# Attention and gated MLP on one core: v's normalization moves from GpSimd to ScalarE, row sums come from the exponential's accumulator, products get a third PSUM bank, and the hand-written order is replaced

## The chip, the core and the metric

The kernel runs on one core of a Trainium2 chip. The metric is device microseconds of one execution. Engines are named as in the profile: PE (TensorE matmul) and PEld (its weight load), DVE (VectorE), ACT (ScalarE), POOL (GpSimd), SP (SyncE, which issues nearly all DMAs).

## The reference

Four batches, 8 heads, 768 positions, 64 columns a head. Attention keeps the first 4 positions (sinks) and a window of 128; its result, 512 columns a row, goes through a gated MLP with a spatial product:

```python
keep = is_sink | in_window
scores = np.where(keep, scale * (q @ k.T), -1e9)
a = np.exp(scores - scores.max(-1)); a = a / (a.sum(-1) + 1e-9)
x = a @ v                                   # heads joined: 512 columns
h = np.maximum(x @ w_in, 0.0)
u, v = h[..., :512], h[..., 512:]
v_n = (v - v.mean(-1)) / np.sqrt(v.var(-1) + 1e-6)
v_s = np.einsum('ts,bsd->btd', w_spatial, v_n) + b_spatial[None, :, None]
out = (u * v_s) @ w_out
```

## The kernel before

A batch has six tiles of 128 positions (`NT`), and each tile two halves of four heads. For each half, `scores` multiplies the queries with the keys of the tile and of the tile before it, 260 columns a head with 2 sink columns on either side (PE into four banks `sc`); DVE adds the mask and takes the row's minimum `nm` (L781); ACT takes the exponential with `nm` as its bias (L786). `weights` splits the result into two fp16 parts `p high` and `p low`, which DMAs turn (`turn high`, `turn low`, L852). `attend` multiplies them with v (`av`: three matmuls for each pair of blocks, L900 to L902). The value tile has a 65th column of ones, so column 65 of each head's product is the row sum. `divide` then reads that column, adds 1e-9, inverts (L908, L909) and multiplies (L910) on DVE. One `av` tile takes two banks, one for each half.

The joined 512 columns `x` are split into two fp16 parts and turned. `v_half` multiplies them with the second half of w_in (`ps_v`), takes the relu, then on DVE mean and variance (`v stats`), on POOL the power -0.5 (`v root`, L1012), and subtracts the mean and multiplies by the root in one instruction (`v norm`, L1015), on POOL or DVE; `vn high` and `vn low` split the result. `u_half` makes u (`ps_u`), `s_piece` the spatial product (`ps_s`), DVE adds the bias (`gate`, L1072), `times` multiplies by u, and `o_piece` multiplies with w_out (`ps_o`). All these products, and the PE transposes `pt` of the first tiles, share two PSUM banks (`mm`). The first two tiles (`crossed`) are computed in fp32, while w_in is still being decoded from its 64-bit form (`w_in`: L548, L550, L553, L556).

Nothing is scheduled by a program: `fast_path` collects 1799 pieces, and the text `ORDER` names them in the sequence in which they are written out, each with its engine (P, d, a, p, S). Each engine runs its own pieces in that sequence. A number behind P (`120P20`) puts that many stand-in matmuls of 248 columns on `ident` ahead of the piece (`warm`, L440). The times given to `plan.add` are not used by the program. In what follows a *score group* is one piece `score`: there are 48.

Of the kernel before, what the change touches and what calls it, by code (L numbers as in the profile page):

```python
# [6 lines left out]
F32 = mybir.dt.float32  # L7
# [6 lines left out]
ALU = mybir.AluOpType  # L14
# [39 lines left out]
def general_path(tc, wf, qk, v, w_in, w_sp, b_sp, w_out, out):  # L54

    nc = tc.nc
    with (
# [46 lines left out]
        for b in range(B):  # L104
            xT = gc.tile([P, DM // P, S], F32, name="g_xT")
            vsb = gc.tile([P, NT, H, D + 1], F32, name="g_v")
            nc.sync.dma_start(vsb, v[b].rearrange("(c p) h d -> p c h d", p=P))
            x = gc.tile([P, NT, DM], F32, tag="g_xg", name="g_x")
            for h in range(H):
# [5 lines left out]
                for t in range(NT):  # L115
# [25 lines left out]
                    for c in range(NT):  # L141
                        nc.tensor.matmul(po[:, :D], prT[:, c, :], vsb[:, c, h, :D],
                                         start=(c == 0), stop=(c == NT - 1))
# [69 lines left out]
BANKS = {"sc": 4, "av": 1, "mm": 2}  # L213
# [8 lines left out]
def cost(e, n, two=False, pointer=False):  # L222

    if e == "a":
        return 0.1 + n / 1200 + (0.1 if pointer else 0)
    if e == "d":
        return 0.085 + n / (960 if two else 1920) + (0.05 if pointer else 0)
    return 0.17 + n * 0.0018 if two else 0.14 + n * 0.001
# [5 lines left out]
116S 120P20 121d 123d 125d 117S 118p 257p 156p 119p 107S 108a 109a 21S 126a 127d 128a 111S 112a 110d 132P6:131  # L234
137d 139d 122a 124a 129P3 135d 22a 23d 133d 113a 136a 24d 25p 209p 114d 155S 159P1:131 164d 162d 140a 166d 130a
138a 134a 42S 141P2 160d 43a 44d 165a 115S 45d 46p 14S 131P 16d 163a 173P 180d 178d 174d 167a 161a 168P 142a 26a
176d 170P 143P 17d 15a 18p 208S 212P 144d 213d 215d 181a 217d 219d 179a 28S 30d 169a 47a 48d 313p 171a 154S 157p
0S 2d 177a 175a 216a 29a 31d 32p 214a 3d 184P15 218a 220a 185a 223a 1a 4p 182P 228P 233d 221a 183d 224d 235d 231d
229d 7S 9d 8a 35S 37d 236a 36a 207S 210a 230a 10d 11p 234a 256S 232a 239a 240p 225d 172P 145P 186P 187d 237a 49S
260P5 261d 38d 146a 50a 51d 39p 311S 314a 267d 33a 12a 188P9 189a 58S 263d 222S 265d 266a 241d 158d 211d 190a  # L240
268a 226S 255S 147P 148a 262a 264a 271a 269a 191d 52d 53p 272p 34d 276P 279d 258a 280a 227P 283d 284a 281d 282a
277d 192P 259d 273d 315d 312S 316P 319d 323d 321d 242S 317d 238S 243P 244d 245P23 278a 285a 289p 332P 287a 288p
5a 360S 6d 54a 40a 41d 27d 55d 270S 274S 275P 324a 322a 318a 339d 320a 193a 325a 286S 290S 246a 503S 327a 19a
333d 337d 340a 338a 334a 199P 326S 335d 247d 361p 364P 329p 328d 330S 336a 343a 344p 341a 13d 20d 504p 505p 345p
367d 368a 365d 200a 371d 369d 291P 56S 359S 292d 149d 342S 150p 151p 201P 346S 202a 380P 381d 550p 366a 370a 372a
373a 377p 57S 387d 383d 385d 382a 384a 194d 195p 293P 386a 294a 295d 375a 196p 248P 376d 508P 515d 513d 331P 509d
511d 374S 63a 64d 378S 249a 152a 388a 391a 203P 392d 549S 347P 389a 390S 393p 204a 153d 394S 348d 516a 250d 510a
512a 205P 206a 522P 296P 527d 523d 525d 349P 362a 363d 65a 251p 524a 66d 379P 529d 528a 526a 514a 517d 519p 297a
298d 652p 299p 197a 350a 530a 351d 67a 198p 553P 560d 561a 531a 558d 559a 556d 554d 555a 303P 395P 304d 533d 501S
506a 68d 557a 252p 253a 254p 567P 574d 568d 569a 396d 570d 603p 300p 572d 59S 69a 70d 352P 353a 518S 507d 520S  # L250
602S 562a 564p 307P 308a 547S 354d 355p 356p 397P 606P 398a 399d 493S 551a 573a 60S 71a 552d 521P 532S 613d 607d
571a 600S 534S 301a 309P 310d 72d 575a 576a 302d 611d 609d 400P 401a 402d 604a 409P 614a 563S 535P 536d 357a 578p
622P 625d 627d 623d 709p 403p 358p 629d 61S 73a 410a 74d 407P 408d 548a 537a 626a 605d 305P 538d 565S 404p 651S
566P 655P 405a 624a 612a 610a 608a 617a 615a 306d 618d 83S 85d 619d 86d 579S 406p 415P 658d 62S 416d 420P 577S
84a 87p 494a 628a 630a 631a 656d 657a 660d 662d 601a 633a 634p 495a 421d 422p 635d 580P 581d 582a 413P 414d 671P
672d 676d 539S 540P 417p 418a 419d 75S 663a 678d 77d 423p 424d 496d 76a 78d 79p 541a 661a 88a 708S 1658a 411P
412a 583d 425P 497S 91S 620S 674d 498a 499a 675a 426d 93d 427d 616S 94d 80a 92a 81d 679a 584S 428a 500d 429d 659a
677a 664a 666a 632S 89d 667p 636S 90a 430P 431d 673a 758p 95p 432p 668d 712P 719d 717d 718a 715d 713d 621P 542d
680a 684p 585P 586a 587d 706S 446P 447d 448p 682a 683d 710a 82p 728P 731d 733d 649S 735d 99S 101d 720a 96a 596P
597a 449a 450d 102d 653d 100a 734a 433a 637P 434d 592P 593a 594P 595a 732a 654d 103p 104a 105d 106p 755S 756a  # L260
441P 442d 729d 451P 736a 650a 98a 757S 761P 900S 901a 730a 665S 97d 443d 588p 669S 589d 590a 638d 711d 759a 760d
444d 438P 739a 740d 452d 453d 502a 670P 737a 741d 681S 685S 439a 902a 903d 440S 435P 738S 1055S 714a 716a 723a
764d 445d 454a 686P 721a 725p 762d 455d 766d 767a 742S 1005S 768d 436a 437S 894S 687d 724p 726S 456P 765a 769a
763a 457d 458d 459a 777P 770d 780d 722S 949S 890S 460d 784d 772a 773p 904p 1061p 639p 778d 782d 785a 781a 783a
953p 477P 743P 467P 774p 478d 468d 469d 598P 905p 775S 771S 479d 480a 895a 779a 788a 470p 471d 908P 913d 911d
599d 909d 915d 896a 897d 543p 640p 1003S 707a 914a 591d 910a 464P 465a 786d 790d 481d 922P 472P 473d 688a 912a
916a 951a 727P 789d 927d 923d 952d 925d 689d 926a 891a 917a 919p 950a 1006a 466S 641S 929d 930a 482P 483d 484d
744d 947S 954a 461P 462a 898S 474p 475d 956P 959d 963d 957d 476d 961d 485a 791S 787S 924a 906d 486d 463S 1009p
544d 745p 776P 1057S 690S 955d 892a 1007a 920S 642P 487P 928a 931p 643a 644d 746d 933p 970P 977d 488a 489S 747S
# [82 lines left out]
def begin(nc, pool, qk, v, w_in, b_sp):  # L352
# [893 lines left out]
```

## Time and profile before

| | |
|---|---|
| median of 3 runs | 401.75 us (401.38 to 401.91) |
| the profiled execution | 401.43 us, of which the profiled span is 399.6 us |
| PE busy | 387.3 us, 97% of the span |
| DVE, ACT, POOL busy | 312.4, 250.8, 210.5 us |
| granted TensorE clock | 0.999 of full speed |

Busy times are sums over the whole span; a matmul's length includes its passage through the array, so matmuls overlap and the pace is read from one start to the next.

### The profile page before, as it was taken

Reading aid. Unit: us, or ns where it says so; the run is one execution under the profiler, and the core shown is the slowest. Engines: PE = TensorE matmul, PEld = TensorE weight load, DVE = VectorE, ACT = ScalarE, POOL = GpSimd, SP = SyncE. Lnnn points to the kernel's source line nnn. Section 1 sums busy time; section 2 is a strip of 40 time slices with the busy share of each in tenths; the row PEclk is TensorE's granted clock in tenths of the full one; section 3 lists DMA queues with packets and bytes.
Section 4 is the critical chain, followed back from the end, with each engine's and each line's share of the span. In section 5 each row is a group of like instructions: output and inputs, shape, how many; then the busy total and the mean of one; then the engine's idle time right before and its main releaser. Section 6 shows DMA issues by size and latency. Waiting matters only on the chain. (4 is left out here: it accounts for less than half of the span.)

```text
span 399.6 us, 9923 instructions
## 1 busy us (share of the span) xinstructions
PE 387.3 (97%) x3697; PEld 276.4 (69%) x3697; DVE 312.4 (78%) x924; ACT 250.8 (63%) x553; POOL 210.5 (53%) x237
## 2 busy tenths in 40 slices
PE   7999998998999999999999999999999998999995
PEld 4785866686786774677777666777768666486773
DVE  3899999879888787989798897989896998342421
ACT  3999897877879476688796979888621131101010
POOL 4463596874552526454515478499666392720000
PEclk9999999999999999999999999999999999999999
DMA  6999999999895998869888979899799653001021
GB/s 194 384 284 218 196 183 230 256 251 219 205 228 135 242 188 192 214 153 144 165 173 210 207 186 267 143 189 147 168 237 232 185 175 85 27 2 53 2 80 57
DMA packets 137733, 70.96 MB, mean 178 GB/s; under 512 B 112080, under 2 KB 125392, under 8 KB 137680
## 3 DMA queue, kind: packets, MB, share of 16 engines
q1 hardware_dynamic: 136864, 70.02, 77.9%
q8 instruction: 30, 0.49, 0.5%
q10 hardware_dynamic: 816, 0.26, 0.3%
q14 instruction: 23, 0.19, 0.2%
HBM read 36.71 MB, written 6.29 MB: 108 GB/s over the span
## 5 line engine op out<-in xcount | busy, mean ns | idle before, releaser
L529 PE MATMUL ps_s<-wsp,vn 128*128 128x256 f16 x864 | 100.3, 273 | 0.7 <-ACT ob L1112 0.7
L786 ACT ACTIVATE pexp<-pexp,nm 128x260 f32<-128x260 f32 (+1 forms) x192 | 85.3, 484 | 18.6 <-DVE nm L781 18.2
L529 PEld LDWEIGHTS <-vn 128*128 128x128 f16 x864 | 83.1, 98 | 14.1 <-issue 2.2
L511 POOL TENSOR_TENSOR p<-pexp,p 128x1024 f16<-128x1024 f32 (+2 forms) x43 | 54.8, 1280 | 44.7 <-ACT p L495 35.7
L529 PE MATMUL ps_u<-xT,win 128*128 128x256 f16 x576 | 68.8, 273 | 1.6 <-DVE g L1072 1.1
L1099 PE MATMUL ps_o<-wout,g 128*128 128x512 f16 x276 | 62.9, 379 | 0.7 <-ACT ob L1112 0.7
L529 PEld LDWEIGHTS <-win 128*128 128x128 f16 x576 | 55.0, 98 | 11.4 <-issue 3.9
L529 PE MATMUL ps_v<-win,xT 128*128 128x512 f16 x264 | 60.5, 380 | 0.1
L1099 PEld LDWEIGHTS <-g 128*128 128x128 f16 x276 | 26.3, 98 | 30.1 <-issue 1.6
L776 PE MATMUL sc<-kring 64*128 64x260 f16 (+3 forms) x480 | 44.7, 312 | 1.3 <-DMA kring<-qk_t 1.2
L529 PEld LDWEIGHTS <-xT 128*128 128x128 f16 x264 | 24.8, 98 | 28.5 <-issue 1.5
L495 ACT CAST p<-pexp 128x32 f16<-128x32 f32 (+2 forms) x69 | 42.7, 639 | 2.7 <-DMA pT<-p 2.0
L1072 DVE SCALAR_TENSOR_TENSOR g<-ps_s,b_bc 128x256 f32<-128x256 f32 x48 | 20.2, 420 | 28.7 <-PE ps_s L529 28.6
L1015 POOL TENSOR_SCALAR vr<-vr,mv,rs 128x512 f32<-128x512 f32 x18 | 38.4, 2136 | 0.8
L1076 POOL TENSOR_TENSOR g<-g,u 128x256 f32<-128x256 f32 x22 | 17.4, 792 | 33.8 <-DVE g L1072 33.1
L1049 ACT ACTIVATE u<-ps_u 128x256 f32<-128x256 f32 x34 | 12.8, 378 | 34.2 <-PE ps_u L529 34.1
L900 PE MATMUL av<-vring,pT 128*128 128x65 f16 x328 | 34.2, 194 | 0.0
L901 PE MATMUL av<-vring,pT 128*128 128x65 f16 x328 | 34.1, 193 | 0.0
L902 PE MATMUL av<-vring,pT 128*128 128x65 f16 x328 | 34.1, 193 | 0.0
L511 DVE TENSOR_TENSOR p<-pexp,p 128x1024 f16<-128x1024 f32 (+2 forms) x33 | 27.0, 820 | 6.3 <-ACT p L495 6.2
L900 PEld LDWEIGHTS <-pT 128*128 128x128 f16 x328 | 30.3, 97 | 1.8 <-issue 0.8
L1084 DVE SCALAR_TENSOR_TENSOR g<-g,g 128x256 f16<-128x256 f16 x48 | 23.0, 484 | 10.0 <-POOL g L679 7.1
(144 smaller groups left out, 693.4 us busy)
## 6 DMA issues: line engine op xcount, KB each, us to landing
vraw<-v_s SPq DMA_DIRECT2D x30, 260.0 KB, 4.1
raw<-qk_t SPq DMA_DIRECT2D x12, 512.0 KB, 4.1
out<-ob SPq DMA_DIRECT2D x23, 256.0 KB, 2.3
kring<-qk_t SPq DMA_DIRECT2D x11, 512.0 KB, 5.6
dec<-w_in SPq DMA_DIRECT2D x8, 512.0 KB, 8.1
pexp<-w_in SPq DMA_DIRECT2D x8, 512.0 KB, 4.4
wsp<-w_sp_t SPq DMA_DIRECT2D x6, 384.0 KB, 4.1
dec<-w_out SPq DMA_DIRECT2D x4, 512.0 KB, 4.6
```

The costliest lines, as they stand in the source:

```text
L495: nc.scalar.copy(o, x)
L511: eng[e].tensor_tensor(out=o, in0=x, in1=hi, op=ALU.subtract)
L529: nc.tensor.matmul(o, a, m, start=(i == 0), stop=(i == n - 1))
L776: nc.tensor.matmul(view(h + q)[0], qq[:, hp, 1, 2:], keys, start=(j == 0), stop=(j == len(pairs) - 1))
L786: nc.scalar.activation(po, po, AF.Exp, bias=nm()[:, q:q + 1], scale=-1.0)
L900: nc.tensor.matmul(o[:, h], ph, vh, start=(t < 2 and j == 0), stop=False)
L901: nc.tensor.matmul(o[:, h], ph, vl, start=False, stop=False)
L902: nc.tensor.matmul(o[:, h], pl, vh, start=False, stop=(j == nb - 1 and (t < 2 or h == HH - 1)))
L1015: eng[e].tensor_scalar(vr(), vr(), vals["mv", i][:, 0:1], vals["rs", i], op0=ALU.subtract, op1=ALU.mult)
L1072: nc.vector.scalar_tensor_tensor(out=g(), in0=tl("ps_s", i)[:, :TC], scalar=G_S, in1=b_bc[:, t0:t0 + TC], op0=ALU.mult, op1=ALU.add)
L1084: plan.add("g low", r, b, "d", cost("d", TC, True), lambda e: nc.vector.scalar_tensor_tensor(out=g2()[:, 1], in0=g2()[:, 0], scalar=-2.0 * ...
L1099: nc.tensor.matmul(o, lead, wout[:, w, d, :], start=(d == 0 and j == 0), stop=(d == KC - 1 and j == 2))
```

## The change

1. The value tiles lose their column of ones (64 columns a head in place of 65). The exponential (now L783) also gives its row sum through ScalarE's accumulator into `sums`. The inverse of the sums is a DVE piece of its own, `den`, which needs no product; `divide` is one multiplication.
2. One `av` tile now fills a single bank with both halves. The bank so freed goes to the products: `mm` has three.
3. `v norm` runs on ACT (`Identity` with a scale and a bias per row) or on DVE, never on POOL. For it, POOL makes `nb`, minus mean times root, behind the root.
4. `ORDER` is replaced as a whole (1815 pieces: 24 `den` more, 8 copies of the ones column fewer). Its stand-ins are 73 in place of 84. It moves work between engines: `v norm` goes from 18 on POOL and 6 on DVE to 20 on ACT and 4 on DVE.
5. At the start, the first keys and queries come in four DMAs of two heads' pairs, alternating between SP's and ACT's queues, in place of two.

```diff
-BANKS = {"sc": 4, "av": 1, "mm": 2}
+BANKS = {"sc": 4, "av": 1, "mm": 3}
...
-116S 120P20 121d 123d 125d 117S 118p 257p 156p 119p 107S 108a 109a 21S 126a 127d 128a 111S 112a 110d 132P6:131
...
+114S 118P16 119d 121d 122a 21S 22a 23d 115S 110S 116p 209p 258p 117p 155p 125d 111a 123d 124a 24d 130P8:141 133d
...
-    st.vring = vring = pool.tile([P, NV, 2, H, D + 1], F16, name="vring")
-    nc.gpsimd.memset(vring[:, :, 0, :, D:], 1.0)
-    nc.gpsimd.memset(vring[:, :, 1, :, D:], 0.0)
...
+    st.vring = vring = pool.tile([P, NV, 2, H, D], F16, name="vring")
...
-            "av": ("av", lambda name: ps_all.tile([P, 2, 512], F32, tag="av", name=name, bufs=1)),
+            "av": ("av", bank("av")),
...
-                nc.scalar.activation(po, po, AF.Exp, bias=nm()[:, q:q + 1], scale=-1.0)
+                k = HH * hf + q
+                nc.scalar.activation(po, po, AF.Exp, bias=nm()[:, q:q + 1], scale=-1.0,
+                                     accum_out=small_tile("sums", (b, t), H)[:, k:k + 1])
...
+            def inverse(e):
+                den = small_tile("sums", (b, t), H)
+                nc.vector.tensor_scalar(den, den, 1e-9, None, op0=ALU.add)
+                nc.vector.reciprocal(den, den)
+
             def divide(e):
-                o = tl("av", (b, t))[:, :, :HH * (D + 1)].rearrange("p s (h d) -> p s h d", h=HH)
-                den = small.tile([P, 2, HH], F32, tag="den", name="den")
-                nc.vector.tensor_scalar(den, o[:, :, :, D], 1e-9, None, op0=ALU.add)
-                nc.vector.reciprocal(den, den)
-                nc.vector.tensor_tensor(out=tl("x", (b, t)), in0=o[:, :, :, :D],
-                                        in1=den.unsqueeze(3).to_broadcast([P, 2, HH, D]), op=ALU.mult)
+                den = small_tile("sums", (b, t), H)
+                nc.vector.tensor_tensor(out=tl("x", (b, t)).rearrange("p s h d -> p (s h) d"),
+                                        in0=tl("av", (b, t)).rearrange("p (h d) -> p h d", h=H),
+                                        in1=den.unsqueeze(2).to_broadcast([P, H, D]), op=ALU.mult)
...
             def root(e):
-                nc.gpsimd.tensor_tensor(out=vals["rs", i], in0=vals["rs", i], in1=mhalf, op=ALU.pow)
+                rs = vals["rs", i]
+                nc.gpsimd.tensor_tensor(out=rs, in0=rs, in1=mhalf, op=ALU.pow)
+                vals["nb", i] = small.tile([P, 1], F32, tag="nb", name="nb")
+                nc.gpsimd.tensor_scalar(vals["nb", i], vals["mv", i][:, 0:1], rs, -1.0, op0=ALU.mult, op1=ALU.mult)
 
             def norm(e):
-                eng[e].tensor_scalar(vr(), vr(), vals["mv", i][:, 0:1], vals["rs", i], op0=ALU.subtract, op1=ALU.mult)
+                if e == "a":
+                    nc.scalar.activation(vr(), vr(), AF.Identity, bias=vals["nb", i], scale=vals["rs", i])
+                else:
+                    nc.vector.tensor_scalar(vr(), vr(), vals["mv", i][:, 0:1], vals["rs", i], op0=ALU.subtract, op1=ALU.mult)
...
-            plan.add("v norm", r, b, "dp", {"d": 0.46, "p": 0.75}, norm, [("st", i)], [("vr", i)], shared=True)
+            plan.add("v norm", r, b, "ad", {"a": 0.61, "d": 0.47}, norm, [("st", i)], [("vr", i)], shared=True)
...
-            for e, hs in ((nc.sync, slice(0, HP // 2)), (nc.scalar, slice(HP // 2, HP))):
-                e.dma_start(kring[:, 0, hs, :, 2:], qk[0, 0, :, hs])
+            for h in range(HP):
+                (nc.sync, nc.scalar)[h % 2].dma_start(kring[:, 0, h:h + 1, :, 2:], qk[0, 0, :, h:h + 1])
```

What the engines' own sequences look like at the places that matter below: first POOL, at the first normalizations of v, before the change. `rs` is the root, `vr` the tile that is normalized, `p` the low part of the softmax weights of one half.

```order
L1012 TENSOR_TENSOR rs<-rs,mhalf 128x1
L1015 TENSOR_SCALAR vr<-vr,mv,rs 128x512
L748 COPY kring<-ksink 128x4x2
L511 TENSOR_TENSOR p_0_130<-pexp,p_0_130 128x1024
L1012 TENSOR_TENSOR rs<-rs,mhalf 128x1
L1015 TENSOR_SCALAR vr<-vr,mv,rs 128x512
L511 TENSOR_TENSOR p_1_131<-pexp,p_1_131 128x1024
```

The same place of POOL in the change:

```order
L509 TENSOR_TENSOR p_1_130<-pexp,p_1_130 128x1024
L1015 TENSOR_TENSOR rs<-rs,mhalf 128x1
L1017 TENSOR_SCALAR nb<-mv,rs 128x1
L740 COPY ksink<-kring 128x16
L744 COPY kring<-ksink 128x4x2 x2
L502 TENSOR_SCALAR p_0_129<-pexp 128x1024
L509 TENSOR_TENSOR vn<-vr,vn 128x512
L509 TENSOR_TENSOR p_0_129<-pexp,p_0_129 128x16
L1015 TENSOR_TENSOR rs<-rs,mhalf 128x1
L1017 TENSOR_SCALAR nb<-mv,rs 128x1
```

The wide instruction behind each root has gone from POOL, a narrow one has come, and a root still stands behind the low part of a half's weights. On ACT the wide one appears between exponentials, as `vr<-vr,nb,rs` (in the change):

```order
L783 ACTIVATE pexp,sums<-pexp,nm 128x260 x2
L493 CAST p_1_130<-pexp 128x1024
L493 CAST p_1_130<-pexp 128x2x16
L1021 ACTIVATE vr<-vr,nb,rs 128x512
L783 ACTIVATE pexp,sums<-pexp,nm 128x128 x4
L1021 ACTIVATE vr<-vr,nb,rs 128x512
L493 CAST p_0_129<-pexp 128x512
```

ACT's queue before the change holds, between exponentials of the same batch, only relus, casts and scaled copies. In the change an ACT instruction that needs POOL's `nb` stands ahead of the next batch's first exponentials (128 columns).

## Rows read from the trace of the kernel before

**Rows 1.** The page: the span, PE's busy time, and its clock in 40 slices.

```profile
span 399.6 us, 9923 instructions
...
PE 387.3 (97%) x3697; PEld 276.4 (69%) x3697; DVE 312.4 (78%) x924; ACT 250.8 (63%) x553; POOL 210.5 (53%) x237
...
PEclk9999999999999999999999999999999999999999
```

**Rows 2.** Waits of PE: who waited for whom: us in total, times, longest.

```profile
PE sc L440 <- POOL ident masks.py:199: 1.7, 1, 1.7
PE sc L776 <- DMA kring<-qk_t: 1.2, 2, 1.0
PE ps_u L529 <- DVE g L1072: 1.1, 1, 1.1
PE pt L815 <- ACT pexp L786: 1.0, 1, 1.0
PE ps_o L1099 <- ACT ob L1112: 0.7, 1, 0.7
PE ps_s L529 <- ACT ob L1112: 0.7, 1, 0.7
PE ps_u L529 <- ACT u L1049: 0.4, 1, 0.4
```

**Rows 3.** Timeline of PE, 102 to 110 us: start, us, instruction.

```profile
102.62 1.15 PE L776 MATMUL sc<-kring 64*128 64x260 f32 x8
103.70 0.28 PE L894 MATMUL av<-vsink,pT 96*128 96x260 f16 x1
103.82 0.20 PE L900 MATMUL av<-vring,pT 128*128 128x65 f16 x1
...
104.55 2.75 PE L529 MATMUL ps_v<-win,xT 128*128 128x512 f16 x12
107.14 2.13 PE L529 MATMUL ps_s<-wsp,vn 128*128 128x256 f16 x18
109.20 1.15 PE L776 MATMUL sc<-kring 64*128 64x260 f32 x8
```

**Rows 4.** Stand-in matmuls: count, busy us, mean ns, idle before.

```profile
L440 PE MATMUL pt<-ident 128*128 128x248 f16 x52 | 6.4, 270 | 0.0
L440 PE MATMUL sc<-ident 128*128 128x248 f16 x25 | 5.0, 382 | 1.7 <-POOL ident masks.py:199 1.7
L440 PE MATMUL av<-ident 128*128 128x248 f16 x7 | 1.1, 271 | 0.0
```

**Rows 5.** Two stretches: length, then busy PE, PEld, DVE, ACT, POOL.

```profile
6.00:49.00 43.00, 41.79 (x377) 30.86 (x376) 39.83 (x138) 39.72 (x86) 18.93 (x21) 1.00 1.05 267
49.00:94.00 45.00, 42.59 (x446) 31.19 (x446) 39.01 (x123) 37.49 (x79) 34.36 (x28) 1.00 1.09 239
```

**Rows 6.** Timeline of ACT: an accumulator read; an exponential and a cast.

```profile
81.92 0.37 ACT L1049 ACTIVATE u<-ps_u 128x256 f32<-128x256 f32 x1
82.19 0.62 ACT L606 ACTIVATE junk<-vraw 128x512 bf16<-128x512 f32 x1
82.71 0.19 ACT L606 ACTIVATION_READ_ACCUMULATOR junk<-vraw 128x1 f32 x1
82.80 0.61 ACT L495 CAST x<-x 128x512 f16<-128x512 f32 x1
...
119.65 0.51 ACT L786 ACTIVATE pexp<-pexp,nm 128x260 f32<-128x260 f32 x1
120.05 0.61 ACT L495 CAST vn<-vr 128x512 f16<-128x512 f32 x1
```

**Rows 7.** Groups of POOL by shape: busy us, mean ns.

```profile
L511 POOL TENSOR_TENSOR p<-pexp,p 128x1024 f16<-128x1024 f32 x20 | 42.2, 2109 | 24.1 <-ACT p L495 24.0
L1015 POOL TENSOR_SCALAR vr<-vr,mv,rs 128x512 f32<-128x512 f32 x18 | 38.4, 2136 | 0.8
L1012 POOL TENSOR_TENSOR rs<-rs,mhalf 128x1 f32<-128x1 f32 x24 | 18.6, 774 | 15.5 <-DVE rs L1009 15.2
```

More of the change, by code (lines that the diff above doesn't have):

```diff
@@ L420, in fast_path @@
             nc.gpsimd.memset(t[:, 4 * HH], 0.0)
-        vsink = [const.tile([96, HH, D + 1], F16, name=f"vsink{i}") for i in range(4)]
+        vsink = [const.tile([96, HH, D], F16, name=f"vsink{i}") for i in range(4)]
         win = const.tile([P, 2, KC, DFF], F16, name="win")
@@ L437, in g @@
                 o = tl(*key[:2])
-                o = o[:, key[2], :248] if key[0] == "av" else o[:, :248]
+                o = o[:, :248]
                 for _ in range(count):
@@ L555, in decode @@
                 [("dec", i)], [("w32", i)], shared=True)
-            plan.add(name, step, 0, "p", 1.27, lambda e: nc.gpsimd.tensor_tensor(
+            plan.add(name, step, 0, "p", 1.23, lambda e: nc.gpsimd.tensor_tensor(
                 out=ci(), in0=ci(), in1=tl("wtmp", i), op=ALU.add), [("wtmp", i)], [("w32", i)])
@@ L614, in check_ranges @@
                 i = ("again", t)
-                load("v check", last, 0, "vraw", i, lambda t=t: v[0, t * P:(t + 1) * P], 260)
+                load("v check", last, 0, "vraw", i, lambda t=t: v[0, t * P:(t + 1) * P], 256)
                 sum_v("v check", last, 0, t, i)
@@ L790, in scores @@
                 keys = [(f"kslot{kslot(0, 0)}", (0, 0), (0, hf))]
-            plan.add("score", i, b, "PE", (0.78 if t else 0.45) if b >= B16 else 1.08 if t else 0.75, product, keys, banks)
+            plan.add("score", i, b, "PE", (0.86 if t else 0.53) if b >= B16 else 1.17 if t else 0.74, product, keys, banks)
             for q in range(n):
@@ L916, in attend @@
             else:
-                plan.add("av", i, b, "PE", 0.0306 * 3 * n + (0.105 if t > 1 else 0.0), product,
+                plan.add("av", i, b, "PE", 0.0302 * 3 * n + (0.104 if t > 1 else 0.0), product,
                          [("pT", i)] + vkeys + ([(f"vsink{vsk}", b)] if t > 1 else []), [("av", (b, t), hf)])
@@ L920, in attend @@
                 return
-            plan.add("divide", i, b, "d", 1.02, divide, [("av", (b, t))], [("x", (b, t))])
+            plan.add("den", i, b, "d", 0.33, inverse, [], [("sums", (b, t))])
+            plan.add("divide", i, b, "d", 0.605, divide, [("av", (b, t)), ("sums", (b, t))], [("x", (b, t))])
             if crossed(b, t):
@@ L948, in split_turned @@
             plan.add("x cross", i, b, "PE", 0.55, cross, [("x", (b, t))], [bank, (*key, t % 2)])
-            plan.add("x high", i, b, "ad", {"a": 0.53, "d": 0.62}, upper, [bank], [(*key, t % 2)])
-            plan.add("x low", i, b, "d", 0.62, lambda e: nc.vector.tensor_tensor(
+            plan.add("x high", i, b, "ad", {"a": 0.508, "d": 0.605}, upper, [bank], [(*key, t % 2)])
+            plan.add("x low", i, b, "d", 0.605, lambda e: nc.vector.tensor_tensor(
                 out=half(1), in0=raw(), in1=half(0), op=ALU.subtract), [bank], [(*key, t % 2)])
@@ L965, in turned @@
             plan.add("x cross", i, b, "PE", 0.55, cross, [("x", (b, t))], [bank, (*key, t % 2)])
-            plan.add("x copy", i, b, "ad", {"a": 0.52, "d": 0.62}, copied, [bank], [(*key, t % 2)])
+            plan.add("x copy", i, b, "ad", {"a": 0.468, "d": 0.605}, copied, [bank], [(*key, t % 2)])
             if t % 2 == 0:
```

244 lines of the change are left out of this document (119 added, 125 removed).

## The prediction

> **What bounds the kernel now.** I read the page first. PE is busy for 387.3 of 399.6 us and its clock stands at the full level in every slice [rows 1]; the other three engines have a fifth to a half of the span free. So I asked next whether PE's busy time is work, and read its timeline from start to start [rows 3]. From 102.62 to 109.20 us everything follows without a hole: twelve matmuls of 512 columns take 2.59 us (216 ns each), eighteen of 256 columns 2.06 us (114 ns each), and 24 `av` matmuls of 65 columns 0.73 us (103.82 to 104.55, 30 ns each; one of the 24 is shown). PE is the bound, and the change leaves the number of its real matmuls as it is. What a change can give back is therefore what PE does besides: waiting, and marking time.
>
> Both are small. The view of waits puts 6.8 us on PE in all that matters here [rows 2]: 1.7 us ahead of the first stand-in, 1.2 us for keys that had not landed, 1.0 us for an exponential, and four waits of 2.9 us together for a PSUM bank that DVE or ACT had not emptied (1.1, 0.7, 0.7, 0.4). The stand-ins take 6.4 + 5.0 + 1.1 = 12.5 us for 84 [rows 4]. All of them stand ahead of the tenth score group: they fill holes in which the operands of the next piece are not ready. Why they were not is seen in the stretches [rows 5]: from 6 to 49 us DVE is busy for 39.8 of 43 us and ACT for 39.7; from 49 to 94 us it is 39.0 and 37.5 of 45. Early on, three engines are full at once, and only after some 94 us does PE alone decide.
>
> **The change part by part.**
>
> *Stand-ins.* 73 in place of 84. Those into `sc` cost 5.0/25 = 0.20 us, the others 7.5/59 = 0.127 us [rows 4]. The new order has 23 of the first kind and 50 of the others: 4.6 + 6.4 = 11.0 us, which is 1.5 us less. This is a gain only if the operands come earlier; if not, the same time shows as waits. Bounds: 0 to -1.5; I take -1.5, for this reason: I counted what stands ahead of the 21st score group (102.62 us) in both orders. PE has the same pieces there, to the last one. ACT has the same 80 exponentials. Each gets an accumulator read, which moves the next start by 0.09 us (82.71 to 82.80), not by its length of 0.19 [rows 6]: 80 x 0.09 = 7.2 us. Six normalizations come to ACT. The trace has none on ACT. By the nearest rows, a 512-column instruction without operands per row steps by 0.52 us (82.19 to 82.71); the exponential with one such operand steps by 0.40 us for 260 columns against 0.27 for 256 without [rows 6], so one operand costs some 0.13 and two at most 0.26: 0.65 to 0.78 us each. I take 0.65: 3.9 us. ACT thus gets 11.1 us. Taken from it ahead of the same place are fourteen instructions of 512 columns (relus of v, casts, decoding), two of 1024, two of 768, two of 256 and four copies of the ones column: 14 x 0.52 + 2 x 1.04 + 2 x 0.78 + 2 x 0.27 + 4 x 0.1 = 11.9 us. ACT's load is unchanged to within a microsecond, and DVE's list there gains seven instructions (four relus of v) and loses eleven, most of them narrower. Neither engine gets new room from the change itself; what the order gains is which of the equal loads come first.
>
> *The third bank.* The four waits for a bank, 2.9 us [rows 2], each fell on a product that needed the bank of the last but one. With three banks the emptying may be a whole product late, 1.3 to 2.6 us at the pace of [rows 3], against waits of at most 1.1. I take all four away: -2.9, bounds 0 to -2.9. The other half of the bargain, `av` in a single bank for both halves, costs nothing: `divide` frees two banks at once before, one now, and no wait of PE for `divide` stands in [rows 2].
>
> *The inverse ahead of `divide`.* The addition and the reciprocal leave the path from `av` to x, but DVE runs them still, and PE waits nowhere for x. I take 0 from 0 to -1.
>
> *Keys.* One key load came 1.0 us late [rows 2]. In SP's new sequence that load (second batch, second tile) stands ahead of two turns of the first batch's last tile; it stood behind them. -1.0, bounds 0 to -1.2.
>
> *The first keys in four DMAs.* The same bytes come in smaller pieces, and 16 stand-ins in place of 20 stand ahead of the first scores. That gain, 4 x 0.20 = 0.8 us, is part of the stand-ins' term; if the keys come no sooner it is a wait at the start. 0 besides.
>
> *Normalization off POOL.* 18 x 2.136 = 38.4 us leave POOL [rows 7]; 24 narrow multiplications `nb` come, at no more than the root's 0.774 each (18.6 us; nothing is nearer in these rows, and a power should be the dearer, so less). POOL was no bound, and PE waits for none of its instructions after the start. 0 on the path; it makes room for the twelve more `times` and the further casts that the order puts there.
>
> *Columns.* By [rows 3] a column costs (216 - 114)/256 = 0.40 ns. 984 `av` matmuls lose one each and 32 sink products four: 1112 columns, -0.4 us; if the weight load sets the pace, 0. The rows at 65 columns (30 ns) lie on the same line as the wide ones: 26 ns for the columns and some 4 ns besides. The Trainium skill, in "TensorE: Matmul & The Clock Gate", section "Back-to-back issue gap", has two readings: its formula (columns over 2.4 GHz, and 2.5 ns) gives 29 ns at 64 columns, its table puts everything up to 64 columns at the issue floor of some 25 ns. By the formula the sum is as here; by the table 984 matmuls would gain some 5 us, as an estimate. No run before shows a 64-column matmul in fp16; the case is a rival below.
>
> *New waits.* Every engine's sequence is another one, and the old sequences kept seven waits after the start, 5.1 us in all [rows 2]. I add one of the mean size: +0.7 (bounds 0 and all of them, +5.1).
>
> Sum: -1.5 - 2.9 - 1.0 - 0.4 + 0.7 = -5.1 us. The profiled execution, 401.43 us (span and 1.8 us around it), would take 396.3; it lies 0.3 under the median of the runs, so I predict 401.75 - 5.1 = 396.7 us.
>
> **The rivals.**
>
> *ACT waits for POOL (slower).* Before, the normalization followed its root on the same engine; it lost 0.8 us in all there [rows 7]. Now ACT's queue stands still until POOL has made `nb`, and POOL's root still stands behind the low part of a half's weights, 2.11 us. At worst a normalization holds ACT for 2.11 + 0.77 + 0.77 = 3.65 us, and behind it stand the next batch's exponentials, for which the turns and then `av` wait. Six of them ahead of the 21st score group cost 21.9 us, against ACT's idle 43 - 39.7 + 45 - 37.5 = 10.8 us: 11.1 us reach PE, and with the gains of 5.1 the time is 407.8. It decides from (10.8 + 5.1)/6 = 2.7 us for each. Against it: the order leaves POOL other work than the root for little of the time, 34.4 of 45 us at most before 38.4 us of normalization left.
>
> *Nothing is won (same).* The operands of the first 50 us come no sooner, since ACT and DVE carry the same load; each stand-in left out becomes a wait, and the waits for banks become waits for what the emptied banks fed. Only the columns remain: 401.3.
>
> *More is won.* The order meets the operands nearly everywhere: no new wait, the exponential's wait of 1.0 gone too, and the small holes besides. PE's idle time is 12.3 us [rows 1], of which [rows 2] names 6.8; half of the other 5.5 would be 2.7. 396.7 - 0.7 - 1.0 - 2.7 = 392.3.
>
> *The 64-column products drop to a floor.* If the 4 ns beside the columns vanish at 64, 984 x 4.4 = 4.3 us: 392.4. For it speaks the table named above and no row; against it the straight line of [rows 3].
>
> **How the numbers follow.** The forecast has 0.60 (393.6 to 399.9, from the bounds: all terms, or half of them), more won 0.15, the floor 0.05, nothing won 0.09, ACT waiting 0.11. Two tenths of a per cent, 0.8 us, is about what a measurement of this kernel can tell from no change. The first three cases are faster (0.80), the fourth is the same, the fifth slower. The range reaches from 391.0, under both cases of more, to 401.3, where nothing is won; it leaves out the slower case and the tails, some 2 in 10.
>
> **What would show it.** PE's groups should have 73 stand-ins and some 11 us for them. The waits of PE for DVE's gate, and ACT's copies of u and out, should be under 1 us together, and no key load should be waited for at the 15th score group. The 21st score group should begin near 100 us; at 102 or later, the start's term failed. `av` starts should lie 30 ns apart; at 25 the floor holds. ACT's accumulator reads should step by 0.09 and its normalizations by 0.65 to 0.78; waits of ACT for POOL's `nb` over 10 us in the first 94 us would mean the slower rival. The forecast is wrong if PE's new waits exceed 6 us, or if `times` and casts on POOL come so late that products wait for them.

## The result, and the profile after

The change makes the kernel slower: 403.25 us (402.55 to 404.18, 7 runs) against 401.38 us of the kernel before on the same chip (399.40 to 402.26, 7 runs); the ratio is 1.0064 with a 95% interval from 1.0043 to 1.0084. The forecast was 396.7 us, with a range from 391.0 to 401.3.

The page of the profiled execution (403.25 us, the span and 1.8 us around it), as [rows 1]:

```profile
span 401.5 us, 10098 instructions
...
PE 388.8 (97%) x3686; PEld 276.6 (69%) x3686; DVE 319.6 (80%) x921; ACT 263.1 (66%) x727; POOL 213.2 (53%) x271
...
PEclk9899999999999999999999999999999999999999
```

The 8 in PE's clock is new: in the second slice TensorE did not run at its full level throughout. This is not the one execution alone: in all 14 of the change (these seven and the seven of `e11_change_again`) the mean granted clock is 0.989 to 0.996, while 79 of the 102 of the kernel before in the later runs have 0.997 or more. PE's waits, to be held against [rows 2] (who waited for whom, total, times, longest):

```profile
PE sc L772 <- DVE nm L777: 1.8, 1, 1.8
PE sc L438 <- POOL ident masks.py:199: 1.7, 1, 1.7
PE ps_u L527 <- DVE g L1080: 0.7, 1, 0.7
PE av L898 <- DMA pT<-p: 0.6, 1, 0.6
PE av L898 <- DVE x L910: 0.5, 1, 0.5
PE ps_s L527 <- DVE g L1080: 0.4, 1, 0.4
```

The waits for late keys and for ACT's copies of `ob` are gone, that for ACT's copies of u is down from 0.4 to 0.2 (not shown); for a gate PE waits 0.7 and 0.4 us, at other places than the 1.1 before. The two stretches of [rows 5]:

```profile
6.00:49.00 43.00, 40.82 (x328) 29.18 (x327) 38.96 (x123) 38.30 (x115) 24.34 (x21) 0.96 0.95 258
49.00:94.00 45.00, 44.16 (x459) 31.78 (x458) 42.50 (x128) 37.65 (x104) 34.62 (x43) 1.00 1.09 233
```

In the two stretches together ACT has about as much to do as before (75.9 us, 77.2 before), DVE 2.6 us more (81.5, 78.8 before), and the clock's mean in the first is 0.96. What stands behind that is a hole at the start. In PE's and DVE's timelines (start, us, instruction, in brackets the idle time before it and what ended it):

```profile
7.75 0.49 PE L772 MATMUL sc<-kring 64*128 64x128 f32 x4
10.08 0.70 PE L772 MATMUL sc<-kring 64*128 64x128 f32 x4 [1.84 <-DVE nm L777]
...
12.68 0.81 PE L772 MATMUL sc<-kring 64*128 64x260 f32 x2
```

```profile
6.30 0.29 DVE L777 CUSTOM_DVE_ANT_0 pexp<-sc,m_first 128x128 f32<-128x128 f32 x1
...
9.39 0.43 DVE L548 TENSOR_SCALAR w<-dec 128x512 int32<-128x512 int32 x1 [2.79 <-DMA dec<-w_in]
9.73 0.28 DVE L777 CUSTOM_DVE_ANT_0 pexp<-sc,m_first 128x128 f32<-128x128 f32 x1
```

The second score group stops in its middle for the masks of the first; DVE has two of these behind the decoding of a piece of w_in, and that waits 2.79 us for its load. The third group then begins at 12.68 us; before, it was 10.67:

```profile
10.67 1.15 PE L776 MATMUL sc<-kring 64*128 64x260 f32 x8
```

Between the hole and the third group the clock falls (a row for each stretch: length, busy time of the engines, then the clock as a share of full speed):

```profile
7.40:10.70 3.30, 1.46 (x12) 0.94 (x10) 1.31 (x6) 0.97 (x2) 0.00 (x0) 1.00 0.83 271
10.80:14.10 3.30, 3.30 (x14) 2.22 (x15) 2.44 (x12) 3.23 (x16) 1.27 (x1) 0.50 1.06 380
```

From 10.8 to 14.2 us TensorE has 1.2 and not 2.4 GHz, after 3.3 us in which it was busy for 1.46. The end is new too. SP's queue (DMA issues) and ACT:

```profile
394.15 0.33 SPq L1154 DMA_DIRECT2D out<-ob  x1
394.54 2.65 SPq L1127 DMA_DIRECT2D out<-ob  x2
397.27 0.38 SPq L1154 DMA_DIRECT2D out<-ob  x1
```

```profile
388.52 0.60 ACT L1120 ACTIVATE ob<-ps_o 128x512 f32<-128x512 f32 x1 [7.28 <-PE ps_o L1107]
```

A tile that ACT finishes at 389.12 us is stored at 394.54 only: in the new order its store stands behind that of a later tile, which waits until 394.1. Three stores come on top of each other, the second of the pair takes 2.1 us to issue, and the last is issued 1.2 us after its tile (396.07). From the last product's start to the end it is now 6.1 us. Before, it was 5.0, with the last store issued as soon as its tile was done:

```profile
395.40 0.67 SPq L1146 DMA_DIRECT2D out<-ob  x1
```

### The profile page after: what moved, and what is told of

It reads as the page before. It is cut to its first block, busy times and chain, and to the rows that moved or that the text cites. A ratio compares the mean times of both kernels' runs of the same rounds, so it can differ in the third digit from the quotient of the medians.

```text
span 401.5 us, 10098 instructions
## 1 busy us (share of the span) xinstructions
PE 388.8 (97%) x3686; PEld 276.6 (69%) x3686; DVE 319.6 (80%) x921; ACT 263.1 (66%) x727; POOL 213.2 (53%) x271
## 4 chain that ended last, share of the span: by engine, by line
PE 58%; DVE 18%; DMA 8%; ACT 7%; issue 4%; POOL 4%; SPq 1%; POOLq 0%; ACTq 0%; DVEq 0%
PE ps_s L527 15%; PE ps_o L1107 10%; PE ps_u L527 10%; PE ps_v L527 9%; PE sc L772 6%; DVE pexp L777 3%; ACT pexp L783 3%; DMA pexp<-w_in 3%; DMA dec<-w_in 2%; PE ps_v L988 2%; DVE kring L516 2%; PE av L898 1%; PE av L900 1%; PE av L899 1%; DMA wsp<-w_sp_t 1%
## 5 line engine op out<-in xcount | busy, mean ns | idle before, releaser
L783 ACT ACTIVATE pexp<-pexp,nm 128x260 f32<-128x260 f32 (+1 forms) x192 | 92.5, 484 | 13.0 <-DVE nm L777 12.2
L509 POOL TENSOR_TENSOR p<-pexp,p 128x16 f16<-128x16 f32 (+2 forms) x43 | 51.2, 1195 | 28.4 <-ACT p L493 17.1
L527 PEld LDWEIGHTS <-win 128*128 128x128 f16 x576 | 54.9, 98 | 12.2 <-issue 3.8
L1084 POOL TENSOR_TENSOR g<-g,u 128x256 f32<-128x256 f32 x34 | 30.9, 908 | 58.8 <-DVE g L1080 46.4
L772 PE MATMUL sc<-kring 64*128 64x260 f16 (+3 forms) x480 | 47.7, 319 | 1.9 <-DVE nm L777 1.8
L493 ACT CAST p<-pexp 128x32 f16<-128x32 f32 (+2 forms) x61 | 34.6, 594 | 3.8 <-DMA pT<-p 3.1
L509 DVE TENSOR_TENSOR p<-pexp,p 128x1024 f16<-128x1024 f32 (+1 forms) x33 | 33.9, 1035 | 4.0 <-ACT p L493 3.4
L1120 ACT ACTIVATE ob<-ps_o 128x512 f32<-128x512 f32 x23 | 13.6, 592 | 35.3 <-PE ps_o L1107 21.5
L783 ACT ACTIVATION_READ_ACCUMULATOR pexp<-pexp,nm 128x1 f32 x192 | 36.3, 189 | 0.0
L898 PE MATMUL av<-vring,pT 128*128 128x64 f16 x328 | 33.1, 193 | 1.2 <-DMA pT<-p 0.6
L900 PE MATMUL av<-vring,pT 128*128 128x64 f16 x328 | 33.1, 193 | 0.0
L899 PE MATMUL av<-vring,pT 128*128 128x64 f16 x328 | 33.0, 193 | 0.0
L898 PEld LDWEIGHTS <-pT 128*128 128x128 f16 x328 | 29.5, 98 | 2.8 <-issue 1.1
L899 PEld LDWEIGHTS <-pT 128*128 128x128 f16 x328 | 29.1, 98 | 0.6
```

Source lines behind the costliest of these rows:

```text
L493: nc.scalar.copy(o, x)
L509: eng[e].tensor_tensor(out=o, in0=x, in1=hi, op=ALU.subtract)
L527: nc.tensor.matmul(o, a, m, start=(i == 0), stop=(i == n - 1))
L772: nc.tensor.matmul(view(h + q)[0], qq[:, hp, 1, 2:], keys, start=(j == 0), stop=(j == len(pairs) - 1))
L783: nc.scalar.activation(po, po, AF.Exp, bias=nm()[:, q:q + 1], scale=-1.0, accum_out=small_tile("sums", (b, t), H)[:, k:k + 1])
L898: nc.tensor.matmul(o[:, h], ph, vh, start=(t < 2 and j == 0), stop=False)
```

## The experiments

Each run is timed against the kernel before on the same chip; ratios are to that kernel, with a 95% interval behind them, and the change's own is 1.0064 (1.0043 to 1.0084). Times of single places come from one profiled execution of each run.

**Decoding behind the masks** (`e1_decode_later`). In `ORDER`:

```diff
-122a 21S 22a 23d 115S ... 124a 24d 130P8:141 ... 131d 25p 26a 112d
+122a 21S 115S ... 124a 130P8:141 ... 131d 22a 23d 24d 25p 26a 112d
```

> The changed kernel, with the decoding of the first piece of w_in (one instruction on ScalarE and two on VectorE, with the two behind them) moved in the order from ahead of the second score group's masks to behind them; nothing else moves. Theory A (the decoding waits for its load and holds the masks, the hole on TensorE at 7.97 us follows, and the clock falls to its lower level for 10.8 to 14.2 us): the 1.8 us wait of the score products for VectorE is gone, the granted clock stays at its upper level from 7.4 us on, the third score group begins near 10.5 us and not at 12.7, and the time is about 3 us under the changed kernel's, a ratio to the kernel before of about 0.999. Rival B (the first loads are late anyway, or later groups wait for the same loads and take the gain back): the third group is earlier but the 15th (63.4 us) is not, the gain is under 1 us, ratio above 1.004.

405.42 us, 1.0141 (1.0081 to 1.0201): by its median slower still than the change, though the two intervals touch, and theory A falls. The hole moved one piece on. ACT stood before the next instruction whose load had not landed, and PE behind ACT:

```profile
ACT vsink L694 <- DMA vsraw<-v_sink: 3.0, 1, 3.0
```

```profile
PE pt L813 <- ACT pexp L783: 4.6, 2, 3.1
```

The clock was at the lower level for 6.8 us. So the place of the decoding is not the cause by itself: another load is late too.

**An earlier store** (`e2_store_earlier`): `1814S 1779S` becomes `1779S 1814S`.

> The changed kernel, with one store of the output (of the tile that ScalarE finishes at 389.1 us) put ahead of the store behind which it stands in SyncE's queue until 394.5. Theory A (three stores crowd into the last microseconds and the last one is issued 1.2 us after its tile is ready): the last store is issued within 0.1 us of its tile, the stretch from the last product's start to the end falls from 6.1 to about 5.0 us, ratio about 1.003. Rival B (the end is set by how long the last bytes take, whatever stands ahead): the stretch stays above 5.8 us, ratio 1.006.

402.41 us, 1.0043 (1.0013 to 1.0073). The stretch at the end was 5.6 us; the last store was issued at once but took 0.94 us to issue. Of the 1.1 us by which theory A wanted the end shorter, 0.5 came, and the interval still holds the change's own ratio: in time it decides nothing. The traces say more: in the six with this store earlier (here and in later runs) the stretch at the end is 4.7 to 5.7 us, in seven without it (the change twice, `e1`, `e3`, `e4`, `e5`, `e7`) 5.6 to 6.2, on the average 0.9 us longer.

**More stand-ins in the hole** (`e3_more_standins`): `130P8:141` becomes `130P26:141`.

> The changed kernel, with 26 stand-in products and not 8 ahead of the second score group, so that TensorE multiplies through most of the 2.0 us hole at 7.97 us while the masks stay as late as they are. Theory A (part of what the start loses is the clock that falls after the hole): the granted clock stays at its upper level between 10.8 and 14.2 us, and the products of that stretch, some 3.4 us at half speed, take about 1.7 us less; ratio about 1.002. Rival B (the groups there wait for masks and exponentials, not for TensorE's speed): the clock stays up, and the third and fifth group begin within 0.5 us of where they began (12.7 and 18.8); ratio 1.005 to 1.007.

402.60 us, 1.0049 (1.0019 to 1.0079). In the profiled execution the clock stays up:

```profile
10.80:14.10 3.30, 2.92 (x21) 1.87 (x21) 3.21 (x16) 3.24 (x16) 1.28 (x2) 1.00 1.07 384
```

The third group begins 0.5 us earlier (12.18), the fifth 0.8 (18.0). Of the start's loss the clock is thus a part: 0.6 us by the ratios, 1.1 at the 21st group of the two traces (102.8 and 103.9), between the two theories.

**Two banks in the new order** (`e4_two_banks`): `"mm": 3` becomes `"mm": 2`.

> The changed kernel with two banks and not three for the products of the feed-forward, in the order that was made for three. By the prediction's term for the third bank (2.9 us of waits that it removes) the time rises by 2.9 us, ratio about 1.0135, and TensorE's waits for the gate on VectorE and the copies on ScalarE rise from 1.3 us by about as much. Rival B (the new order, not the bank, removed those waits): under 0.7 us, ratio under 1.008. Rival C (the new order lives on the third bank more than the old one wanted it): over 6 us, ratio over 1.021.

436.49 us, 1.0876 (1.0823 to 1.0928), rival C. PE waits for banks in many places, the most here:

```profile
PE ps_o L1107 <- DVE g L1080: 4.5, 4, 1.7
```

The run shows what the new order needs, not what a third bank would give the old one; that was not run.

Then the loads. SP's queue in the change, up to the third group's key load, and SP's wait ahead of it:

```profile
0.72 0.96 SPq L1198 DMA_DIRECT2D kring<-qk_t  x2
1.74 0.46 SPq L521 DMA_DIRECT2D dec<-w_in  x1
2.24 0.43 SPq L521 DMA_DIRECT2D vsraw<-v_sink  x1
3.81 0.68 SPq L736 DMA_DIRECT2D kring<-qk_t  x1
```

```profile
SPq L736 <- DMA kring<-qk_t: 1.1, 1, 1.1
```

SP holds this load for 1.1 us, until another load has landed. The landings in the trace are counted by eight semaphores, which the program gives to its loads in rotation, and the ninth load is issued 0.02 us after the first load with the same semaphore (the first on ACT's queue, which counts with SP's) has landed: in the change at 3.81 and 3.79 us, before at 5.06 and 5.04, in the two runs below at 4.93 and 4.91, 3.92 and 3.90. Before, the first keys took two of the eight, and the third group's key load was the eighth, issued at 2.70 and landed at 10.53; the wait fell on the load behind it:

```profile
2.70 0.67 SPq L740 DMA_DIRECT2D kring<-qk_t  x1
```

```profile
SPq L523 <- DMA kring<-qk_t: 1.7, 1, 1.7
```

With four it is the ninth: issued at 3.81, landed at 12.16.

**Two key loads in the change** (`e5_two_key_loads`) **and four in the kernel before** (`e6_before_four_loads`). The edit of the first; the second has it the other way round:

```diff
-            for h in range(HP):
-                (nc.sync, nc.scalar)[h % 2].dma_start(kring[:, 0, h:h + 1, :, 2:], qk[0, 0, :, h:h + 1])
+            for e, hs in ((nc.sync, slice(0, HP // 2)), (nc.scalar, slice(HP // 2, HP))):
+                e.dma_start(kring[:, 0, hs, :, 2:], qk[0, 0, :, hs])
```

> The changed kernel, with the first keys in two loads as before and not in four; the order stays that of the change. In the traces a load waits until the one issued eight loads earlier has landed: before, the third group's key load is the eighth and is issued at 2.70 us and landed at 10.5; after, it is the ninth, issued at 3.81, landed at 12.2. Theory C (the two added loads push every later load one rotation back): it is issued by 2.8 us, lands by 11.2, the third group begins near 11 us and not at 12.7, and the time falls by 1 to 2 us, ratio 0.9995 to 1.003. Rival A (the masks behind the decoding are the cause, whatever the loads): the hole at 8 us stays, the third group begins after 12 us, gain under 0.5 us, ratio over 1.004.

> The kernel before, with the first keys in four loads and nothing else of the change. Theory C: its third group's key load is issued at 3.8 us and not 2.7 and lands near 12, the third group begins near 12.2 and not at 10.7, and the time rises by 1 to 2 us, ratio 1.0025 to 1.005. Rival (the prediction's own term: no cost besides earlier first keys): within 0.3 us, or faster by what the first group gains, ratio 0.998 to 1.001.

401.44 us, 1.0021 (1.0002 to 1.0040), and 401.18 us, 1.0028 (1.0006 to 1.0051). Both ratios lie where theory C put them: 0.4% given back in the one, some 0.3% lost in the other. In the change with two loads, SP issues the third group's key load at 2.24 us, and PE begins that group at 10.51:

```profile
2.24 0.67 SPq L736 DMA_DIRECT2D kring<-qk_t  x1
```

```profile
10.51 1.15 PE L772 MATMUL sc<-kring 64*128 64x260 f32 x8 [0.97 <-DVE pT L817]
```

The third group follows its keys: it begins 0.14 us after they have landed in the kernel before, here and with the 26 stand-ins (10.53, 10.37 and 12.04 us), 0.25 after in the kernel before with four loads (11.47). The hole is gone though the decoding still stands ahead of the masks: its load lands at 6.18 us and not at 9.36, and the clock stays up. For this load the eight semaphores are not the reason. It is the fifth in the change and waits for none; it is issued 0.5 us later than with two loads (1.74, not 1.23) and lands 3.2 us later (8.9 to 9.6 us in the seven traces of this order with four loads, 6.1 to 7.7 in the five with two and the decoding in its place). That two loads more ahead of it cause this is shown by the runs; how they do is open. In the kernel before, with four loads, the key load is issued at 4.29 us as the tenth, and the third group begins later:

```profile
11.72 1.15 PE L776 MATMUL sc<-kring 64*128 64x260 f32 x8
```

That is 1.05 us later than before, but at the 21st group only 0.16 is left of it (102.78 and 102.62): the 1.1 us for which PE waited for a gate near 92 us [rows 2] is gone in this trace, since the delay has taken its place. So the trace shows the late start and does not show where the 0.3% is lost.

**No accumulator** (`e7_no_accumulator`). The row sums are left out; a constant is inverted:

```diff
-                nc.scalar.activation(po, po, AF.Exp, bias=nm()[:, q:q + 1], scale=-1.0,
-                                     accum_out=small_tile("sums", (b, t), H)[:, k:k + 1])
+                nc.scalar.activation(po, po, AF.Exp, bias=nm()[:, q:q + 1], scale=-1.0)
...
-                nc.vector.tensor_scalar(den, den, 1e-9, None, op0=ALU.add)
+                nc.vector.memset(den, 64.0)
```

> The changed kernel without the accumulator on the 192 exponentials: the row sums are left out, and a constant stands where they are inverted. It takes 192 reads of 0.093 us, 17.9 us, off ScalarE. Theory (ScalarE has room, as predicted; the reads cost nothing on the path): time within 0.8 us of the changed kernel, ratio 1.0045 to 1.008. Rival D (the reads make ScalarE late, and the new waits of TensorE come from there): at least 2 us less, ratio under 1.0015, and TensorE's waits for exponentials and copies of ScalarE shrink.

403.03 us, 1.0059 (1.0037 to 1.0081). 17.9 us less on ACT bring nothing that can be measured: ACT has room for the reads.

**Start and end by hand** (`e8_start_and_end`): two key loads, the store, 26 stand-ins, and

```diff
-114S 118P16 119d 121d 122a 21S 22a 23d 115S ... 125d 111a 123d 124a 24d 130P8:141
+114S 118P16 119d 121d 122a 154S 21S 115S ... 125d 123d 124a 130P26:141
...
-131d 25p 26a 112d 128d 154S 158P ... 138a 132a 139P1
+131d 128d 22a 23d 24d 25p 158P ... 138a 132a 111a 112d 26a 139P1
```

> The changed kernel with its start and its end mended together: the first keys in two loads, the third group's key load first in the queue behind them, the decoding of the first piece of w_in and the first sink of v behind the second group's masks and exponentials, 26 stand-ins ahead of the second group, and the store that stood behind a later one put ahead of it. Theory A with C: the third group begins by 10.5 us, the clock stays at its upper level, the fifth group begins by 17 us (16.6 before, 18.8 after), and the time is 2.5 to 3.5 us under the changed kernel's: ratio 0.998 to 1.0005. Rival B (later waits take it back): the 21st group is no earlier than 103.0 and the ratio stays above 1.003.

401.68 us, 1.0029 (1.0009 to 1.0048), no better than two loads alone: rival B by the 21st group, just under its 1.003 by the ratio. The third group begins at 10.5, the clock holds, but the fifth begins at 18.1 and the 21st at 104.8: what was moved back came late for others. The profiled execution, 403.99 us, is the slowest of the twelve, so these places are its worst case.

```profile
PE av L892 <- DMA pT<-p: 1.8, 1, 1.8
```

**Two key loads and the earlier store** (`e9_loads_and_store`), **two steps of DVE moved besides** (`e10_two_waits_less`), **and the change again** (`e11_change_again`), on one chip. Of the second, in `ORDER`:

```diff
-1488d 891d 1392S 1394S 1447a 1362d
+1362d 1488d 891d 1392S 1394S 1447a
...
-1586d 1692d 1693S 1275P 1276d
+1275P 1276d 1586d 1692d 1693S
```

> The changed kernel with the first keys in two loads and the late store ahead of the one it stood behind; nothing else. If the two repairs add up (1.0064 to 1.0021 by the loads, 0.5 us off the end by the store): ratio 0.9995 to 1.0015, the third group begins at 10.5, the stretch from the last product's start to the end is 5.6 us or less. Rival (the store's place is worth nothing in the time): ratio 1.0015 to 1.003 and the end stays at 6.1 us.

> As the run with two loads and the earlier store, and two steps of VectorE moved: the division of one pair of score groups ahead of two other steps (TensorE waits 0.70 us for it near 246 us), and one gate ahead of a division and of a sum of the weights' check (TensorE waits 0.89 us near 307 us). Theory (the new waits come from where VectorE's order puts these steps, not from how much it has to do): both waits go and the time is 1.0 to 1.6 us under that run, a ratio of about 0.996 to 0.998. Rival (VectorE is full there, the steps put back make the next product late): one or both waits come back within 5 us of their place, gain under 0.4 us.

> The changed kernel as it is, beside the two mended ones on the same chip. Ratio 1.005 to 1.008 to the kernel before; the granted clock falls to its lower level for one or two stretches between 9 and 17 us as in its first profile, the third group begins after 12 us, the stretch at the end is above 6 us. If instead it comes out under 1.004, the gain of the repairs is smaller than the ratios of different chips say.

399.95 us, 1.0002 (0.9981 to 1.0023); 401.10 us, 1.0026 (1.0006 to 1.0045); 403.25 us, 1.0068 (1.0038 to 1.0099). The two repairs add up: 403.25 - 399.95 = 3.3 us less than the change, with intervals apart, and level with the kernel before. The stretch at the end is 4.8 us, with the stores apart:

```profile
392.85 0.33 SPq L1154 DMA_DIRECT2D out<-ob  x1
393.71 0.33 SPq L1127 DMA_DIRECT2D out<-ob  x1
394.80 0.53 SPq L1154 DMA_DIRECT2D out<-ob  x1
```

Moving DVE's steps does not help; the rival holds. Near 247 us PE's wait of 0.54 us for the division is gone, and at 248.8 PE waits 1.03 us for a copy of u on DVE. Near 307 us, in the run with two repairs and then in the one with the gate moved:

```profile
308.07 1.14 PE L527 MATMUL ps_u<-xT,win 128*128 128x256 f16 x9 [0.73 <-DVE g L1080]
```

```profile
304.94 2.78 PE L527 MATMUL ps_u<-xT,win 128*128 128x256 f16 x24
309.04 1.24 PE L527 MATMUL ps_v<-win,xT 128*128 128x512 f16 x5 [1.32 <-DVE g L1080]
```

`ps_u` runs through, and the next product waits 1.32 us for the next gate.

**Less work on DVE** (`e12_no_inverse`, `e13_no_small_addend`): the kernel with the two repairs, and in `inverse` both steps left out (x is scaled by the sum), or the first alone:

```diff
-                nc.vector.tensor_scalar(den, den, 1e-9, None, op0=ALU.add)
-                nc.vector.reciprocal(den, den)
```

> The kernel with two loads and the earlier store, without the inverse of the row sums: its two small steps on VectorE (0.20 and 0.12 us, 24 times, 7.7 us) are left out, and the product is scaled by the sum itself. Theory (TensorE's new waits for masks, gates and divisions come from VectorE having no room where they fall): the score groups with added waits (1.4 to 1.5 us at the 8th, 18th to 20th, 42nd) come down toward 1.08 and 0.77 us, and the time falls by 1 us or more, ratio under 0.998. Rival (they come from the places in the order, whatever VectorE's load): under 0.4 us, ratio 0.999 to 1.002.

> The kernel with two loads and the earlier store, without the addition of 1e-9 to the row sums ahead of their inverse (0.20 us on VectorE, 24 times, 4.8 us; the largest term of each sum is 1, so the sum is the same). Theory as in the run without the inverse, at 4.8 us in place of 7.7: 0.6 us or more off, ratio under 0.999. Rival: within 0.3 us, ratio 0.9995 to 1.002.

399.86 us, 0.9990 (0.9970 to 1.0010), and 400.19 us, 0.9987 (0.9964 to 1.0011). Against 1.0002 that is some 0.5 us, on another chip and with intervals that overlap. The times do not decide: the smaller cut meets its theory's bounds (0.6 us, under 0.999), the larger one its rival's (0.999 to 1.002). Of the stretched score groups the 42nd went back to 0.77 us without the inverse and the 18th to 1.08; the 19th and 20th stayed at 1.40 and 1.50, the 8th at 1.59 (from 1.52), and the 12th and 16th rose to 1.26 and 1.38. So DVE's amount of work explains a part at most; the rest is left to the places of the steps, for which the section below shows one place in the trace, but no run that moves it.

## Why the prediction was wrong, point by point

**"The first keys in four DMAs ... 0 besides."** This step failed first. The prediction looked at what the four loads bring and not at the loads behind them. To the first group they bring nothing: it begins at 5.13 us in the new order with four loads and with two, and at 5.98 in the old order with two and with four, so the 16 or 20 stand-ins ahead of it, and not the loads, go with its start. And they cost: the third group's key load has to wait for a semaphore and lands 1.8 us later than with two loads (12.16, not 10.37), the decoding's load 3.2 us later; the masks behind the decoding, the hole and the clock follow. That is about 0.43% or 1.7 us of the change (1.0064 to 1.0021). The clock by itself is the smaller part of it (0.6 us by the run with 26 stand-ins). SP's wait of 1.7 us ahead of the ninth load, shown above, was in the trace before.

**The end.** The prediction had no term for it. One store that stands behind a later one in SP's queue costs up to 0.8 us (1.0021 to 1.0002, on two chips and with intervals that overlap; 0.9 us by the average of the traces). What is queued behind a waiting DMA issue was in the order for both kernels to be read.

**"New waits: +0.7."** Mis-sized by far, and the reason why nothing is won once the two repairs are made. In the repaired kernel's trace (`e9`) I add, for each kind of product, the times from one start to the next, take out the idle time between products, and compare with the kernel before:

| from start to start, us | before | repaired | difference |
|---|---|---|---|
| stand-ins | 11.7 | 10.2 | -1.5 |
| `av` | 40.2 | 39.1 | -1.1 |
| `ps_o`, `ps_s`, `ps_v`, `ps_y`, `ps_row` | 223.5 | 222.9 | -0.6 |
| score groups | 41.5 | 43.8 | +2.3 |
| `ps_u` | 63.9 | 64.8 | +0.9 |
| `pt` | 6.2 | 6.1 | -0.1 |
| idle between products | 5.9 | 5.3 | -0.6 |

The stand-ins give the 1.5 us of the forecast, the narrower `av` 1.1 and not 0.4. But the list of waits after the start holds 5.1 us again, as [rows 2] does, where the sum left 1.9 (5.1 - 2.9 - 1.0 + 0.7). That is 3.2 us too much, and another 3.2 us stand in score groups and `ps_u` that take longer without a wait in the list: with the 0.7 some 7 us of new waits, over the 6 us that the prediction named as a sign of being wrong. Eight score matmuls at one place of the repaired kernel take

```profile
88.19 1.46 PE L772 MATMUL sc<-kring 64*128 64x260 f32 x8
```

where [rows 3] has 1.15, and PE counts as busy all through, because a matmul's length reaches over the start of the next. What they wait for stands in DVE's timeline:

```profile
87.35 0.85 DVE L509 TENSOR_TENSOR vn<-vr,vn 128x512 f16<-128x512 f32 x1
88.12 0.42 DVE L777 CUSTOM_DVE_ANT_0 pexp<-sc,m_even 128x260 f32<-128x260 f32 x1
...
88.47 0.42 DVE L777 CUSTOM_DVE_ANT_0 pexp<-sc,m_even 128x260 f32<-128x260 f32 x1
```

Two masks of the group before still have to empty their `sc` banks, behind a split of `vn`; the last ends at 88.89, and the sixth of the eight starts behind it at 88.95, though the fifth, beside which it runs elsewhere, started at 88.73. At the 42nd group it is a gate that stands between the masks. At the 18th it is the product behind the scores that is late: a `ps_u` starts at 84.12, when DVE has emptied a bank of `ps_v` (84.07). That these places come from the new order and not from DVE's load is likely after the runs without the inverse, but no run moved a mask.

**"The third bank ... I take all four away: -2.9."** By the list of waits, 2.9 us for a bank fell to 1.5 (u on ACT and on DVE 0.2 each, the gate 0.7 and 0.4); in the repaired kernel it is 1.9, and the late `ps_u` above is one more, which the list does not name. The single bank for `av` was taken to cost nothing; PE now waits 0.5 us there for the division that empties it. The rival that nothing is won, given 0.09, has the outcome of the repaired kernel; its mechanism (waits for banks become other waits) is there in part. The change itself came out slower, but not by the mechanism of the slower rival: that was given 0.11, and no run tested it beyond the waits told below.

**What held, and how far.** The stand-ins:

```profile
L438 PE MATMUL sc<-ident 128*128 128x248 f16 x23 | 4.4, 367 | 1.7 <-POOL ident masks.py:199 1.7
L438 PE MATMUL pt<-ident 128*128 128x248 f16 x24 | 3.9, 292 | 0.0
L438 PE MATMUL av<-ident 128*128 128x248 f16 x12 | 2.1, 330 | 0.0
L438 PE MATMUL ps_v<-ident 128*128 128x248 f16 x14 | 1.8, 269 | 0.0
```

Their number, 73, is as forecast; they are busy for 12.2 us, where 11.0 were forecast (12.5 before), with some at the lower clock, and for 11.5 with two loads and the store. The key load at the 15th score group is no longer waited for. The prices on ACT:

```profile
101.06 0.19 ACT L783 ACTIVATION_READ_ACCUMULATOR pexp<-pexp,nm 128x1 f32 x1
101.15 0.58 ACT L1001 ACTIVATE vr<-ps_v 128x512 f32<-128x512 f32 x1
...
119.19 0.80 ACT L1021 ACTIVATE vr<-vr,nb,rs 128x512 f32<-128x512 f32 x1
119.89 1.04 ACT L495 ACTIVATE kring<-raw 128x1024 f16<-128x1024 f32 x1
```

A read steps by 0.09 us and a normalization by 0.70, inside 0.65 to 0.78. ACT's waits for `nb` were 1.0 us in the first 94 (7.6 over the whole span), a tenth of the 10 us that were to mean the slower rival. `nb` takes 0.451 us of POOL on the average, under the bound of 0.774.

The 64-column products, 24 starts from the first of these rows to `ps_v`, are 0.70/24 = 29 ns apart: the formula that the Trainium skill gives in "TensorE: Matmul & The Clock Gate", section "Back-to-back issue gap", holds (29 ns), and the table's floor of some 25 ns does not reach up to 64 columns here.

```profile
105.06 0.19 PE L898 MATMUL av<-vring,pT 128*128 128x64 f16 x1
...
105.76 2.75 PE L527 MATMUL ps_v<-win,xT 128*128 128x512 f16 x12
```

The 21st group began at 103.86 us, and at 102.44 in the repaired kernel; the prediction had said that at 102 or later the start's term failed. Before, it was 102.62, so nothing is gained up to there.

## What to carry to other kernels

A load that is split takes more of a fixed number of completion semaphores (eight here): count which load the split makes wait, and what waits for that one, before calling it free. In an order written by hand, read what stands behind each instruction that waits, at the very start and the very end first, where nothing covers it. A list of waits is no sum of what can be won. Here one engine was busy for 97% of the span, and waits that were taken away came back at other places where a feeding engine was late; part of them stood in no list, and only the times from start to start showed them.

## What the hardware did that was not expected

- Near the end a DMA issue on SP mostly takes 0.33 us, but 2.1 us when it follows two others within 0.9 us (394.15, 394.54, 395.06); in all seven traces with the late store the third of three so close took 1.3 to 2.1 us. The last one took 0.94 in the run with the store alone moved.
- After a stretch of 3.3 us with PE busy for 1.46 the clock went to 1.2 GHz; with 26 stand-ins in the same stretch (busy 3.18) it stayed at 2.4. In the six traces with a hole near that place (the change twice, and the runs `e1`, `e2`, `e4` and `e7`) the lower level lasted 3.4 us twice and 6.8 us four times.
- Two banks in place of three cost the new order 33 us, eleven times the 2.9 us of waits for which the prediction wanted the third bank.
